# Output projection of a recurrent segment loop: its last blocks by column halves, and the segment's end spread over the next step

## The chip, the cores and the metric

The kernel runs on one core of a Trainium2 chip, whose engines are TensorE (matmuls and transposes, into PSUM), VectorE, ScalarE, GpSimd and SyncE, the last of which here only issues DMA transfers. Time is device time in microseconds (us) of one execution; the figure quoted for a kernel is the median of its runs.

## The reference, cut to what matters

Two independent parts are computed and set side by side in the output's columns. Part B is a long convolution (state space model); it comes first in the kernel and is not touched. Part A is an attention layer that runs over segments, and each segment needs the result of the one before:

```python
for s in range(n_seg):                                  # 64 segments of 32 rows
    h = jnp.concatenate([mem, x[:, 32*s:32*s+32]], axis=1)   # 8 memory rows + 32 rows, 1024 wide
    q, k, v = (einsum('btd,dhe->bhte', h, W) for W in (Wq, Wk, Wv))   # 32 heads of 128
    p = softmax(where(mask, einsum('bhqe,bhke->bhqk', q, k) * scale, -1e9))
    o = einsum('bhte,hed->btd', einsum('bhqk,bhke->bhqe', p, v), Wo)
    mem = o[:, :8]                                      # memory of the next segment
    outs.append(o[:, 8:])
```

All data are bf16, sums are kept in f32.

## The kernel before

**The recurrent rows.** Only 32 of a segment's 40 rows depend on the loop: the 8 memory rows and 24 of the 32 others are the columns of `hT` (1024 as 8 blocks of 128 partitions, 32 columns each; columns 24 to 31 hold the memory). The remaining 8 rows of each segment ("left") have their keys, queries and values made ahead of the loop and kept in DRAM (`PKd`, `VXd`); what the attention gives for them (the left products) is written to `OLd` in each step and projected after the loop, for all segments at once.

**One step.** `part_a` (L233) runs 64 steps. The order of all instructions on every engine is written out by hand in the source: each engine executes its instructions in that order, and waits where data is not there. A step projects K, Q of the first half of the heads (t = 0), K, Q of the second (t = 1), then V of both (`quads`, L358: eight blocks of weights each; four matmuls of 512 columns run side by side on four column groups of TensorE); ScalarE copies each result from PSUM to SBUF (`evac`, L369). Between them stand the transposes of K and Q (`tr`, L374), the scores (L387), the softmax (`below`, `powers`, `weigh`, `turn`, L404 to L425, VectorE and ScalarE), the spreading of the probabilities over block-diagonal tiles (L427 to L440, VectorE and GpSimd) and the product with V (`pv`, L442). `evac_o` (L458) copies that product to `o0` and `o1`, and `oproj` (L467) multiplies it with the sixteen blocks of Wo, blocks 0 to 7 from `o0`, 8 to 15 from `o1`. An even block reads the first half of `o0` or `o1` (two of its four heads), an odd block the second half. The sum stands in `pp[:, 1, :]`, as four row groups of 256 columns.

**The end of a step (L563 to L583).** ScalarE copies the sum to `ob` in two halves of 128 columns (L567), TensorE forms the left product of t = 1 (`pv_l`), then transposes both halves (L573), VectorE writes the memory columns of `hT` from them (L575), even 128-blocks of `hT` from the first half and odd ones from the second. The next step's first matmul (block 0 of K) needs `hT`. Then VectorE fetches the weight block `("k", 0, 7)`, and ScalarE copies the two left products (L578, L581), with the load of the next step's `PKd` rows (L327) between them, and issues two stores (L343, L347).

**Weights.** Most of the 64 blocks of 512 KB are resident in SBUF. Twelve are streamed from DRAM in every step by SyncE's queue through four slots (`stage`, L294): `STREAM` names nine, `STREAM_O` blocks 4, 8, 13 of Wo. A slot is reloaded as soon as TensorE has read it for the last time. Three blocks (`KEPT`: K 7, half of Q 7, half of Wo 15) live in PSUM as raw bits and are fetched by VectorE into SBUF in each step (`fetch`, L311; `words`, L291), in pieces of at most 512 columns.

**The arena.** Almost all of a step's small tiles share one SBUF area of 5984 bytes a partition. `AT` gives each tile's byte address; tiles whose lives do not overlap lie on each other, and a write into a place waits for the reads of what lay there.

Of the kernel before, what the change touches and what calls it, by code (L numbers as in the profile page):

```python
# [11 lines left out]
F32 = mybir.dt.float32  # L12
# [20 lines left out]
SLOTS = 4  # L33

ARENA = 5984
AT = {"K7a": 3072, "K7b": 1024, "K7c": 2048, "K7d": 4192, "ob": 4960, "pk": 0, "vx": 3392, "Q7a": 2048, "Q7b": 3072,
# [3 lines left out]


def weight_blocks(Wq, Wk, Wv, Wo):
# [190 lines left out]
def part_a(ctx, tc, x, src, WD, HE, seg_len, out_a, ahead, W_res, rest, places, first):  # L233
# [27 lines left out]
    def unit(key):  # L261
        if key in rest:

            rest.remove(key)
            load_resident(tc, wres, src, key, W_res, None, places.pop(0)() if places else None)
        if key in W_res:
            return W_res[key]
        if key in KEPT:
            return ahead_of.pop(key) + halves.get(key, [])
        between.pop(key, lambda: None)()  # L270
        if key in first:
            return first.pop(key)
        return stage(key, WD[key][:])
# [8 lines left out]
    def at(name, *dims):  # L282

        n = int(np.prod(dims))
        t_ = arena[:, AT[name] // 2:AT[name] // 2 + n]
        if len(dims) == 1:
            return t_
        names = "abc"[:len(dims)]
        return t_.rearrange("p (%s) -> p %s" % (" ".join(names), " ".join(names)), **dict(zip(names, dims)))

    def words(out, in_):  # L291
        nc.vector.tensor_scalar(out=out.bitcast(I32), in0=in_.bitcast(I32), scalar1=0, scalar2=None, op0=ALU.bitwise_or)  # L292
# [7 lines left out]
    def load_kept(key):  # L300
        t_ = first.pop(key) if key in first else stage(key, src(key))
        kept[key] = {}
        for n in (1,) if key in HALF else (0, 1):
            kept[key][n] = ps_k.tile([128, 512], F32, name="keep", tag="keep%d" % sum(len(b) for b in kept.values()))
            words(kept[key][n][:], t_[:, 1024 * n:1024 * n + 1024])
        if key in HALF:
            t_ = ahead.low["half"] if key[0] == "q" else wres.tile([128, 1024], BF16, name="Whalf")
            nc.sync.dma_start(out=t_[:], in_=src(key)[:, 0, :] if key[0] == "o" else src(key)[:, 0:1024])
            halves[key] = [(0, 1024, t_)]

    def fetch(key):  # L311

        ahead_of[key] = []
        for name, lo, n in KEPT[key]:
            t_ = at(name, n) if name else S_[:, 0:n]
            words(t_, kept[key][lo // 1024][:, lo % 1024 // 2:(lo % 1024 + n) // 2])
            ahead_of[key].append((lo, n, t_))

    def columns(w, lo, n):

        if not isinstance(w, list):
            return [(0, w[:, lo:lo + n])]
        return [(max(lo, l_) - lo, t_[:, max(lo, l_) - l_:min(lo + n, l_ + n_) - l_]) for l_, n_, t_ in w if l_ < lo + n and lo < l_ + n_]

    def load_pk(j):
        pk = at("pk", 512)
        nc.scalar.dma_start(out=pk, in_=PKd[j])  # L327
        return pk
# [23 lines left out]
    load_kept(("k", 0, 7))  # L352
    fetch(("k", 0, 7))
    pk = load_pk(0)
    between["q", 0, 2] = lambda: load_kept(("q", 0, 7))
    between["v", 0, 7] = lambda: load_kept(("o", 15))
    for s in range(NS):
        def quads(m, t, kcs, a=None):  # L358
            if a is None:
                a = ps.tile([128, 512], F32, name="acc", tag=BANK[m, t])  # L360
            for kc in kcs:
                w = unit((m, t, kc))
                for g in range(4):
                    for o_, rhs in columns(w, 512 * g, 512):
                        nc.tensor.matmul(a[32 * g:32 * g + 32, o_:o_ + rhs.shape[1]], lhsT=hT[:, kc, :], rhs=rhs,  # L365
                                         start=(kc == 0), stop=(kc == KC - 1), tile_position=(0, 32 * g), skip_group_check=True)
            return a
# [87 lines left out]
            pv(p[:], t, V, pb.rearrange("p a b c -> p a (b c)"), lbs)  # L455
            return p

        def evac_o(p, name):  # L458
            o = at(name, 4, 4, SL)
            nc.scalar.copy(out=o, in_=p[:].rearrange("p a (g q) -> p a g q", g=4))  # L460
            return o

        def pv_l(pl, t, V, L):

            pv(pl, t, V, L[:, 0].rearrange("p (a b) k -> p a (b k)", a=4), [L[:, 1].rearrange("p a k -> p (a k)")])

        def oproj(po, us, oT):  # L467
            for u in us:
                w = unit(("o", u))
                for hh in range(2):  # L470
                    h = 2 * u + hh
                    for qt in range(4):
                        for o_, rhs in columns(w, 1024 * hh + 256 * qt, 256):
                            nc.tensor.matmul(po[32 * qt:32 * qt + 32, o_:o_ + rhs.shape[1]], lhsT=oT[:, h % 4, (h % 16) // 4, :], rhs=rhs,  # L474
                                             start=False, stop=(h == 31), tile_position=(0, 32 * qt), skip_group_check=True)

        a = quads("k", 0, (0, 2, 4, 6, 1, 3, 5, 7))
        k0 = evac(a, "k0")
        a = quads("q", 0, range(0, 6))
        fetch(("q", 0, 7))  # L480
# [74 lines left out]
        powers(sc1, 1)  # L555
        oproj(pp[:, 1, :], range(0, 5), o0)
        pv1 = pv_x(1, V1, pb1, [lb1])
        o1 = evac_o(pv1, "o1")
        lt1 = turn(weigh(sc1, 1, "ln1"), "lt1")
        oproj(pp[:, 1, :], range(5, 8), o0)  # L560
        L1 = left_blocks(lt1[:, 0:4, :], lt1[:, 4, :], "L1")
        fetch(("o", 15))
        oproj(pp[:, 1, :], range(8, 16), o1)  # L563
        ob = at("ob", 2, 256)
        osb = ob[:, 0, :]
        for j in range(2):
            nc.scalar.copy(out=osb[:, 128 * j:128 * j + 128], in_=pp[:, 1, 128 * j:128 * j + 128])  # L567
        pl = ps.tile([128, 4, 32], F32, name="pl", tag="b2")
        pv_l(pl[:], 1, V1, L1)
        if s + 1 < NS:  # L570
            pt_o = [ps.tile([128, 4, SL], BF16, name="tro", tag=tag) for tag in ("b0", "b1")]
            for j in range(2):
                nc.tensor.transpose(out=pt_o[j][:].rearrange("p a b -> p (a b)"), in_=osb[:, 128 * j:128 * j + 128], identity=ident[:])  # L573
            for j in range(2):
                nc.vector.tensor_copy(out=hT[:, :, XM:SL].rearrange("p (q j) r -> p j q r", j=2)[:, j], in_=pt_o[j][:, :, XM:SL])  # L575
        if s + 1 < NS:
            fetch(("k", 0, 7))
        nc.scalar.copy(out=ob[:, 1, 0:128], in_=pp[:, 0, 0:128])  # L578
        if s + 1 < NS:
            pk = load_pk(s + 1)  # L580
        nc.scalar.copy(out=ob[:, 1, 128:256], in_=pl[:].rearrange("p a k -> p (a k)"))  # L581
        if s + 1 < NS:
            stores(s, ob)  # L583

    order = sorted(range(16), key=lambda u: ("o", u) not in W_res)
    wo = {}
# [933 lines left out]
```

## Time and profile before

| | |
|---|---|
| median of 3 runs | 2079.41 us (2068.97 to 2083.44) |
| the profiled execution's own time | 2084.53 us |
| its span, first to last instruction | 2082.8 us |
| mean granted TensorE clock | 0.978, 1.00 from 800 to 2000 us |
| DMA: moved in all | 590.77 MB, 284 GB/s on average |
| streamed loads of the loop (wst from WD) | 768 blocks of 512 KB |
| PKd and VXd loads, OLd and out stores in each step | 128, 112, 64 and 64 KB |

How to read the lines that follow. PE is TensorE, PEld its weight loads, DVE VectorE, ACT ScalarE, POOL GpSimd, SP SyncE; a "q" behind a name is the issue of a DMA on that engine. L12 is line 12 of the kernel. Groups of lines name output and input tiles, partitions x elements and type. A line of the timeline has its start in us, its length, engine, line, operation, tiles, count, and in brackets how long the engine had been idle before and which instruction ended that. The chain of work that ended last follows each instruction back to what released it. The busy time of stretches gives each engine's busy us in each stretch in the order PE, PEld, DVE, ACT, POOL, then granted clock, DMA share, GB/s. A line of the waits has the waiting engine and line, what ended the wait, us in total, times, the longest.

The loop fills the time from about 700 to 2020 us; what lies before is part B and the making of the left rows' keys and values, what lies after the projection of the left products.

### The profile page before, as it was taken

Reading aid. Unit: us, or ns where it says so; the run is one execution under the profiler, and the core shown is the slowest. Engines: PE = TensorE matmul, PEld = TensorE weight load, DVE = VectorE, ACT = ScalarE, POOL = GpSimd, SP = SyncE. Lnnn points to the kernel's source line nnn. Section 1 sums busy time; section 2 is a strip of 40 time slices with the busy share of each in tenths; the row PEclk is TensorE's granted clock in tenths of the full one; section 3 lists DMA queues with packets and bytes.
Section 4 is the critical chain, followed back from the end, with each engine's and each line's share of the span. In section 5 each row is a group of like instructions: output and inputs, shape, how many; then the busy total and the mean of one; then the engine's idle time right before and its main releaser. Section 6 shows DMA issues by size and latency. Waiting matters only on the chain.

```text
span 2082.8 us, 78569 instructions
## 1 busy us (share of the span) xinstructions
PE 1877.7 (90%) x33734; PEld 1188.9 (57%) x33734; DVE 1417.1 (68%) x3352; ACT 1047.5 (50%) x1917; POOL 402.5 (19%) x780
## 2 busy tenths in 40 slices
PE   2699999978999679999999999999999999999989
PEld 1365665756888435555555555555555555555554
DVE  8689999889899246665656656666566666666650
ACT  5899999951333234444444444444444444444430
POOL 2133443452010111111111111111111111111121
PEclk9999999989999779999999999999999999999999
DMA  7696985665635799999999999999999999999991
GB/s 192 179 255 205 266 234 167 167 207 185 217 131 179 288 339 341 343 339 336 336 328 325 334 327 344 337 335 340 331 342 343 336 340 345 334 341 345 332 334 49
DMA packets 344017, 590.77 MB, mean 284 GB/s; under 512 B 108536, under 2 KB 220184, under 8 KB 341620
## 3 DMA queue, kind: packets, MB, share of 16 engines
q1 hardware_dynamic: 297016, 528.00, 74.5%
q0 software_dynamic: 10544, 33.69, 4.8%
q10 hardware_dynamic: 36108, 24.07, 3.7%
q8 instruction: 264, 4.33, 0.8%
q14 instruction: 85, 0.70, 0.1%
HBM read 530.86 MB, written 65.26 MB: 286 GB/s over the span
## 4 chain that ended last, share of the span: by engine, by line
PE 34%; DMA 23%; DVE 4%; issue 2%; ACT 2%; POOL 0%; ACTq 0%; SPq 0%; POOLq 0%; DVEq 0%
PE acc L365 20%; PE pp L474 6%; DMA wst<-WD_o 6%; DMA wst<-WD_v 5%; DMA arena<-PKd 5%; DMA wst<-WD_q 3%; PE pe L610 3%; DMA wst<-WD_k 2%; PE tr L376 2%; PE sc L390 1%; DMA W_o<-in_A_Wo_dram 1%; DVE arena L432 1%; ACT arena L460 1%; DVE sc L407 1%; PE pv L444 0%
## 5 line engine op out<-in xcount | busy, mean ns | idle before, releaser
L365 PEld LDWEIGHTS <-a_hT 128*32 128x32 bf16 x12352 | 342.3, 96 | 302.4 <-issue 56.6
L371 ACT CAST arena<-acc 128x512 bf16<-128x512 f32 x384 | 225.1, 586 | 408.0 <-PE acc L365 348.8
L365 PE MATMUL acc<-W,a_hT 128*32 128x512 bf16 x4864 | 377.1, 383 | 0.3 <-issue 0.3
L474 PEld LDWEIGHTS <-arena 128*32 128x32 bf16 x8256 | 210.3, 97 | 107.7 <-ACT arena L460 52.1
L365 PE MATMUL acc<-wst,a_hT 128*32 128x512 bf16 x2304 | 232.7, 383 | 23.8 <-DMA wst<-WD_v 11.3
L292 DVE TENSOR_SCALAR arena<-keep 128x256 int32<-128x256 int32 (+1 forms) x512 | 176.3, 396 | 39.5 <-PE acc L365 36.8
L474 PE MATMUL pp<-W_o,arena 128*32 128x256 bf16 x4608 | 174.3, 275 | 6.5 <-DMA W_o<-in_A_Wo_dram 6.2
L365 PE MATMUL acc<-MF,a_hT 128*32 128x512 bf16 x2048 | 172.3, 383 | 0.0
L379 POOL COPY arena<-arena 128x128 bf16<-128x128 bf16 x128 | 37.6, 294 | 685.9 <-DMA arena<-PKd 309.9
L414 DVE TENSOR_REDUCE a_mx<-sc 128x4 f32<-128x160 f32 (+1 forms) x192 | 73.0, 380 | 82.2 <-ACT sc L410 82.2
L167 PE MATMUL pro<-xTl,wsl 128*128 128x512 bf16 x512 | 119.0, 383 | 9.5 <-ACT xTl L111 5.1
L406 DVE TENSOR_REDUCE a_mx<-sc 128x4 f32<-128x160 f32 (+1 forms) x192 | 71.9, 375 | 78.9 <-PE sc L394 77.6
L1059 PEld LDWEIGHTS <-MF 128*128 128x128 bf16 x1024 | 102.8, 101 | 30.1 <-issue 8.7
L410 ACT ACTIVATE sc<-sc 128x160 f32<-128x160 f32 (+1 forms) x192 | 63.9, 333 | 102.6 <-DVE sc L407 80.1
L437 POOL TENSOR_TENSOR arena<-arena,a_BD 128x128 bf16<-128x128 bf16 x128 | 69.2, 541 | 226.5 <-DVE arena L424 209.8
L489 DVE COPY arena<-tr 128x512 bf16<-128x512 bf16 x64 | 27.2, 425 | 126.0 <-PE tr L376 126.0
L1059 PE MATMUL hps<-KT,MF 128*128 128x256 bf16 x720 | 94.7, 284 | 14.2 <-DVE x L1228 11.2
L567 ACT CAST arena<-pp 128x128 bf16<-128x128 f32 x128 | 27.8, 269 | 154.9 <-PE pp L474 154.9
L1285 PE MATMUL yp<-Bt,MI 128*128 128x256 bf16 x680 | 104.5, 275 | 0.8 <-ACT yb L1301 0.8
L460 ACT CAST arena<-pv 128x512 bf16<-128x512 f32 x128 | 75.3, 588 | 56.7 <-PE pp L444 42.4
L1097 ACT ACTIVATE E<-pa 128x648 bf16<-128x648 f32 x128 | 91.4, 714 | 17.0 <-PE pa L1089 10.1
L474 PE MATMUL pp<-wst,arena 128*32 128x256 bf16 x1536 | 76.9, 277 | 19.6 <-DMA wst<-WD_o 11.8
(314 smaller groups left out, 3971.8 us busy)
## 6 DMA issues: line engine op xcount, KB each, us to landing
wst<-WD_v SPq DMA_DIRECT2D x256, 512.0 KB
wst<-WD_k SPq DMA_DIRECT2D x192, 512.0 KB
wst<-WD_o SPq DMA_DIRECT2D x192, 512.0 KB
wst<-WD_q SPq DMA_DIRECT2D x128, 512.0 KB
Ud<-ux POOLq DMA_DIRECT2D x16, 1024.0 KB, 5.4
uq<-Ud SPq DMA_DIRECT2D x32, 512.0 KB
wsl<-in_A_Wk_dram SPq DMA_DIRECT2D x16, 512.0 KB
wsl<-in_A_Wv_dram SPq DMA_DIRECT2D x16, 512.0 KB
```

The source lines that it names most:

```text
L167: nc.tensor.matmul(a[:], lhsT=w[:, kc, 128 * j:128 * j + 128], rhs=xTl[:, kc, :, :].rearrange("p s k -> p (s k)"), start=(kc == 0), stop=( ...
L292: nc.vector.tensor_scalar(out=out.bitcast(I32), in0=in_.bitcast(I32), scalar1=0, scalar2=None, op0=ALU.bitwise_or)
L365: nc.tensor.matmul(a[32 * g:32 * g + 32, o_:o_ + rhs.shape[1]], lhsT=hT[:, kc, :], rhs=rhs, start=(kc == 0), stop=(kc == KC - 1), tile_pos ...
L371: nc.scalar.copy(out=q, in_=a[:])
L406: nc.vector.tensor_reduce(out=m_, in_=x, axis=AX.X, op=ALU.max)
L414: nc.vector.tensor_reduce(out=m_, in_=x, axis=AX.X, op=ALU.add)
L437: nc.gpsimd.tensor_tensor(out=L[:, 0].rearrange("p (a b) k -> p a b k", a=4), in0=bc(lt[:, :, 0:XL].unsqueeze(2), [128, 4, 4, XL]), in1=bc ...
L460: nc.scalar.copy(out=o, in_=p[:].rearrange("p a (g q) -> p a g q", g=4))
L474: nc.tensor.matmul(po[32 * qt:32 * qt + 32, o_:o_ + rhs.shape[1]], lhsT=oT[:, h % 4, (h % 16) // 4, :], rhs=rhs, start=False, stop=(h == 3 ...
L1059: pe.matmul(s_[r][half][:, cs, :], lhsT=MF[:, kc, 4 * rr + mc, cs, :], rhs=rhs, start=(i == 0 and mc == 0), stop=(i == 1 and mc == 3), ski ...
L1097: sc.activation(out=T["E", r, e // 4][:, lo:lo + 8 * NE].rearrange("p (i c) -> p i c", i=2), in_=T.pop(("p", r, e))[:, :, 0:4 * NE], func= ...
L1285: pe.matmul(yp[:, b, :], lhsT=m_[:, b, cs, kc, :], rhs=Bt[:, kc, j, half, c_, :], start=(kc == 0 and cs == 0 and half == 0), stop=(kc == 3 ...
```

## The change

The last three blocks of Wo (now 11, 13, 15) are multiplied by column halves. Columns 0 to 127 go to `pp` as before; columns 128 to 255 go to a tile of their own in another PSUM bank (`rest_o`), and what the earlier blocks had summed there is copied to SBUF (`base`, f32) and added by VectorE. Blocks of the second half of the heads run in the order 8, 10, 12, 14, 9, then 11, 13, 15, and `o1` is copied in two halves. The first half of the result is transposed at the end of the step; the second (`memory(1)`) in the next step, behind the first block of K, in a tile shared with the left product of t = 1 (`last`). The left products are copied, and the two stores issued, in the next step too. The block `("k", 0, 7)` is fetched by ScalarE in its last three pieces, and by VectorE in the first two, one ahead of and one behind `memory(1)`; the load of `PKd` stands behind ScalarE's pieces. All arena tiles have new places.

```diff
-AT = {"K7a": 3072, "K7b": 1024, "K7c": 2048, "K7d": 4192, "ob": 4960, "pk": 0, "vx": 3392, "Q7a": 2048, "Q7b": 3072,
-      "k0": 1024, "q0": 3328, "KT0": 2048, "QT0": 1024, "k1": 1024, "q1": 4288, "pn0": 5312, "pt0": 2304, "KT1": 1024,
-      "QT1": 4288, "pb0": 4448, "V0": 1024, "L0": 5472, "o0": 2048, "V1": 1024, "pn1": 3072, "pt1": 4288, "pb1": 0,
-      "lb1": 4960, "ln1": 0, "lt1": 704, "L1": 2048, "o1": 3936, "Oa": 4960, "Ob": 2560}
+AT = {"K7a": 3072, "K7b": 0, "K7c": 4864, "K7d": 4096, "ob": 2048, "pk": 1024, "vx": 4352, "Q7a": 3072, "Q7b": 4960,
+      "k0": 0, "q0": 4352, "KT0": 3072, "QT0": 0, "k1": 3072, "q1": 0, "pn0": 2048, "pt0": 5344, "KT1": 3072, "QT1": 0,
+      "pb0": 3072, "V0": 2048, "L0": 0, "o0": 3072, "V1": 0, "pn1": 5248, "pt1": 5664, "pb1": 1024, "lb1": 2048,
+      "ln1": 2048, "lt1": 2368, "L1": 3072, "o1": 4960, "Oa": 1024, "Ob": 3584}
...
+    def fetch_bits(eng, key, pieces):
+        for name, lo, n in pieces:
+            t_ = at(name, n) if name else S_[:, 0:n]
+            bits = kept[key][lo // 1024][:, lo % 1024 // 2:(lo % 1024 + n) // 2]
+            if eng is nc.vector:
+                words(t_, bits)
+            else:
+                eng.copy(out=t_, in_=bits.bitcast(BF16))
+            ahead_of[key].append((lo, n, t_))
...
+    def memory(j):
+        nc.tensor.transpose(out=tr_o[j].rearrange("p a b -> p (a b)"), in_=osb[:, 128 * j:128 * j + 128], identity=ident[:])
+        nc.vector.tensor_copy(out=hT[:, :, XM:SL].rearrange("p (q j) r -> p j q r", j=2)[:, j], in_=tr_o[j][:, :, XM:SL])
+
+    def left_out():
+        nc.scalar.copy(out=ob[:, 1, 128:256], in_=last[:, 0:128])
+        nc.scalar.copy(out=ob[:, 1, 0:128], in_=pp[:, 0, 0:128])
...
-        def evac_o(p, name):
-            o = at(name, 4, 4, SL)
-            nc.scalar.copy(out=o, in_=p[:].rearrange("p a (g q) -> p a g q", g=4))
+        def evac_o(p, name, parts=1):
+            o, n = at(name, 4, 4, SL), 4 // parts
+            for i in range(0, 4, n):
+                nc.scalar.copy(out=o[:, i:i + n], in_=p[:, i:i + n, :].rearrange("p a (g q) -> p a g q", g=4))
             return o
...
+        def oblock(po, u, w, oT, lo, n, start=False):
+            for hh in range(2):
+                h = 2 * u + hh
+                for qt in range(4):
+                    for o_, rhs in columns(w, 1024 * hh + 256 * qt + lo, n):
+                        nc.tensor.matmul(po[32 * qt:32 * qt + 32, o_:o_ + rhs.shape[1]], lhsT=oT[:, h % 4, (h % 16) // 4, :], rhs=rhs,
+                                         start=start and hh == 0, stop=(h == 31), tile_position=(0, 32 * qt), skip_group_check=True)
...
-        a = quads("k", 0, (0, 2, 4, 6, 1, 3, 5, 7))
+        a = quads("k", 0, (0,))
+        if s:
+            fetch_bits(nc.vector, ("k", 0, 7), KEPT["k", 0, 7][0:1])
+            memory(1)
+            fetch_bits(nc.vector, ("k", 0, 7), KEPT["k", 0, 7][1:2])
+            left_out()
+            stores(s - 1, ob)
+        quads("k", 0, (2, 4, 6, 1, 3, 5, 7), a)
...
-        o1 = evac_o(pv1, "o1")
+        o1 = evac_o(pv1, "o1", 2)
...
         fetch(("o", 15))
-        oproj(pp[:, 1, :], range(8, 16), o1)
+        oproj(pp[:, 1, :], (8, 10, 12, 14, 9), o1)
         ob = at("ob", 2, 256)
-        osb = ob[:, 0, :]
-        for j in range(2):
-            nc.scalar.copy(out=osb[:, 128 * j:128 * j + 128], in_=pp[:, 1, 128 * j:128 * j + 128])
-        pl = ps.tile([128, 4, 32], F32, name="pl", tag="b2")
-        pv_l(pl[:], 1, V1, L1)
+        osb, base = ob[:, 0, :], ob[:, 1, :].bitcast(F32)
+        ends = [(u, unit(("o", u))) for u in (11, 13, 15)]
+        for u, w in ends:
+            oblock(pp[:, 1, 0:128], u, w, o1, 0, 128)
+        nc.scalar.copy(out=osb[:, 0:128], in_=pp[:, 1, 0:128])
+        nc.scalar.copy(out=base, in_=pp[:, 1, 128:256])
+        rest_o = ps.tile([128, 128], F32, name="po", tag="b2")
+        for u, w in ends:
+            oblock(rest_o[:], u, w, o1, 128, 128, u == 11)
+        last = ps.tile([128, 512], F32, name="pl", tag="b1")
         if s + 1 < NS:
-            pt_o = [ps.tile([128, 4, SL], BF16, name="tro", tag=tag) for tag in ("b0", "b1")]
-            for j in range(2):
-                nc.tensor.transpose(out=pt_o[j][:].rearrange("p a b -> p (a b)"), in_=osb[:, 128 * j:128 * j + 128], identity=ident[:])
-            for j in range(2):
-                nc.vector.tensor_copy(out=hT[:, :, XM:SL].rearrange("p (q j) r -> p j q r", j=2)[:, j], in_=pt_o[j][:, :, XM:SL])
+            tr_o = [ps.tile([128, 4, SL], BF16, name="tro", tag="b0")[:], last[:, 256:320].bitcast(BF16).rearrange("p (a b) -> p a b", a=4)]
+            memory(0)
+        pv_l(last[:, 0:128].rearrange("p (a k) -> p a k", a=4), 1, V1, L1)
+        nc.vector.tensor_tensor(out=osb[:, 128:256], in0=rest_o[:], in1=base, op=ALU.add)
         if s + 1 < NS:
-            fetch(("k", 0, 7))
-        nc.scalar.copy(out=ob[:, 1, 0:128], in_=pp[:, 0, 0:128])
-        if s + 1 < NS:
+            ahead_of["k", 0, 7] = []
+            fetch_bits(nc.scalar, ("k", 0, 7), KEPT["k", 0, 7][2:])
             pk = load_pk(s + 1)
-        nc.scalar.copy(out=ob[:, 1, 128:256], in_=pl[:].rearrange("p a k -> p (a k)"))
-        if s + 1 < NS:
-            stores(s, ob)
+        if s + 1 == NS:
+            left_out()
```

More of the change, by code (lines that the diff above doesn't have):

```diff
@@ L465, in pv_l @@
             pv(pl, t, V, L[:, 0].rearrange("p (a b) k -> p a (b k)", a=4), [L[:, 1].rearrange("p a k -> p (a k)")])
+        def oblock(po, u, w, oT, lo, n, start=False):
[5 more added lines that the diff above has]
+                                         start=start and hh == 0, stop=(h == 31), tile_position=(0, 32 * qt), skip_group_check=True)
         def oproj(po, us, oT):
             for u in us:
[L469 to L475, printed above, removed]
-        a = quads("k", 0, (0, 2, 4, 6, 1, 3, 5, 7))
+                oblock(po, u, unit(("o", u)), oT, 0, 256)
+        a = quads("k", 0, (0,))
[6 more added lines that the diff above has]
+        quads("k", 0, (2, 4, 6, 1, 3, 5, 7), a)
         k0 = evac(a, "k0")
```

## The prediction

> **What bounds the kernel now.** First the page: busy shares, slices, the chain that ended last.
>
> ```profile
> PE 1877.7 (90%) x33734; PEld 1188.9 (57%) x33734; DVE 1417.1 (68%) x3352; ACT 1047.5 (50%) x1917; POOL 402.5 (19%) x780
> DMA  7696985665635799999999999999999999999991
> PE 34%; DMA 23%; DVE 4%; issue 2%; ACT 2%; POOL 0%; ACTq 0%; SPq 0%; POOLq 0%; DVEq 0%
> PE acc L365 20%; PE pp L474 6%; DMA wst<-WD_o 6%; DMA wst<-WD_v 5%; DMA arena<-PKd 5%; DMA wst<-WD_q 3%; PE pe L610 3%; DMA wst<-WD_k 2%; PE tr L376 2%; PE sc L390 1%; DMA W_o<-in_A_Wo_dram 1%; DVE arena L432 1%; ACT arena L460 1%; DVE sc L407 1%; PE pv L444 0%
> ```
>
> From slice 15 on (the loop of 64 segments, 62 full steps of 20.02 us on average by the starts in the trace) the DMA row stands at 9, and the chain alternates between matmuls (L365, L474) and loads: streamed weights, and the small PKd load. Three stretches of the loop, each engine's busy time, then clock, DMA share and rate:
>
> ```profile
> 800.00:1200.00 400.00, 376.92 (x8442) 220.40 (x8445) 248.84 (x775) 177.89 (x398) 57.58 (x138) 1.00 0.95 334
> 1200.00:1600.00 400.00, 379.64 (x8536) 223.57 (x8532) 250.98 (x784) 178.52 (x400) 57.61 (x141) 1.00 0.95 337
> 1600.00:2000.00 400.00, 380.34 (x8539) 223.28 (x8531) 250.14 (x783) 178.75 (x403) 59.23 (x142) 1.00 0.95 338
> ```
>
> TensorE and the DMA engines are both at 95%: a step moves 6.73 MB, which at a share of 1.00 would take 0.947 x 20.02 = 18.96 us. So neither alone sets the step. By phase of the step the DMA share is 0.97 to 1.02 in the third to the twelfth twentieth and 0.87 to 0.94 in the last seven: up to the scores of t=1 the loads are late, after them a chain of engines sets the pace. The end of one step shows that chain (start, us, engine, line, idle before):
>
> ```profile
> 1219.33 0.31 DVE L406 TENSOR_REDUCE a_mx<-sc 128x4 f32<-128x160 f32 x1
> 1220.04 0.29 ACT L410 ACTIVATE sc<-sc 128x160 f32<-128x160 f32 x1 [1.14 <-DVE sc L407]
> 1220.43 0.59 ACT L460 CAST arena<-pv 128x512 bf16<-128x512 f32 x1
> 1221.07 0.40 PE L474 MATMUL pp<-wst,arena 128*32 128x256 bf16 x8 [0.24 <-ACT arena L460]
> 1221.76 0.65 DVE L292 TENSOR_SCALAR arena<-keep 128x256 int32<-128x256 int32 x2
> 1222.33 0.21 DVE L292 TENSOR_SCALAR a_S<-keep 128x64 int32<-128x64 int32 x1
> 1222.78 0.22 PE L474 MATMUL pp<-a_S,arena 128*32 128x128 bf16 x1
> 1223.09 0.27 ACT L567 CAST arena<-pp 128x128 bf16<-128x128 f32 x1 [2.07 <-PE pp L474]
> 1223.15 0.32 ACTq L327 DMA_DIRECT2D arena<-PKd  x1
> 1223.41 0.40 PE L573 MATMUL tro<-a_ident,arena 128*128 128x128 bf16 x2
> 1223.68 0.34 DVE L575 COPY a_hT<-tro 128x32 bf16<-128x32 bf16 x2 [1.14 <-PE tro L573]
> 1223.90 0.40 PE L365 MATMUL acc<-Wlow,a_hT 128*32 128x512 bf16 x4
> ```
>
> VectorE's maxima (L406) release the exponential, ScalarE then copies o1 in one piece (L460), and TensorE takes up the output blocks 0.64 us after that copy begins. VectorE meanwhile fetches block 15 from PSUM (L292). After the last output matmul (1222.78) TensorE does little for 1.12 us: copy at +0.30, transposes at +0.62, hT copy at +0.89, next step's first matmul at +1.12. One more wait matters:
>
> ```profile
> POOL arena L379 <- DMA arena<-PKd: 303.6, 46, 7.7
> ACT arena L567 <- PE pp L474: 136.5, 60, 3.8
> ```
>
> In 46 of 60 steps the packed K/Q rows (PKd) land last of all that GpSimd's put_kl (L379) waits for. Issued 0.75 us ahead of the step's first matmul, they land 5.04 us behind it on average, and the scores (L390) can start 0.49 us later; that cost TensorE 0.11 us a step.
>
> [...] both L573 stand between L448 and L365, each in order. [...] PKd lands 0.17 us after the streamed block k1:5 that was issued 0.54 us before it, and over 55 steps the two landings correlate at 0.93. [...] L437 takes 0.40 us alone and 0.77 beside VectorE's L432/L429; L429 then 0.55 instead of 0.42.
>
> **The change part by part**, per step. E is the last output matmul of before; times in ScalarE's and VectorE's order are counted from the last matmul of the left half (in before, from E). I take the spacings of before's instructions, over all steps of the trace.
>
> *o1 by halves.* ScalarE copies 512 columns in 0.59 us, 128 in 0.27; by the line between them 256 take 0.38. The four even units need only the first half, so TensorE resumes 0.21 us earlier; the second half ends at 0.75, long before the unit that needs it (four units of 0.218 us later). **-0.21**.
>
> *Column halves.* A group of four 256-column matmuls starts every 109 ns, one of 128 columns every 56 ns (the last two L474 of the step), so splitting adds 3 ns to six groups, **+0.02**. The six groups of the right half (0.34 us) now run behind the left half's copy (0.62 us from its last matmul to the transposition): **-0.34** at best. pv_l, 0.23 us, stays under cover of the hT copy.
>
> *What holds these two back.* Already the left half of unit 15 needs VectorE's second piece (Ob). It ends at E-0.25 in the median step, never later than E-0.18, while TensorE would come to it at E-0.60. Taking for each step the later of E-0.59 and the end of Ob plus 0.07, the left half's last matmul comes 0.31 us before E on average: 0.12 in the 29 of 63 steps where VectorE sets it, up to 0.59 in those delayed by loads. Then L0: its new place lies on QT1, so GpSimd starts it after the scores, beside VectorE's L429; by the contended row that delays VectorE by 0.12 us, in half the steps, 0.06 on average. Gain of the end: 0.31 - 0.06 = **-0.25**.
>
> *The right half's transposition in the next step.* The median gap into a group of transposes is 0.312 us where 0.213 is the stream before it, and out of it 0.149: 0.25 us of TensorE for one. **+0.25**. Its operand (the addition: after the hT copy at +0.89, spacing 0.17, and 0.33 as L417, the nearest row) is there at about +1.40 of the left half's end; TensorE asks at 1.12 + 0.31 = 1.43. Odd blocks are read three units later (0.64 us), VectorE's K7a piece (0.38) and the hT copy fit in. Cover gone, each 0.1 us late is 0.1 us of step.
>
> *K7's last three pieces on ScalarE, left_out and stores in the next step.* ScalarE: copies at 0.30 and 0.46, K7c from 0.70 to 1.19, K7d to 1.57, the last to 1.84, the two left products to about 2.4, two store issues (0.33 and 0.57) to about 3.4; k0's copy is due at 3.45. It is hidden by k0's own eight units; if not, the tr(k0) that waits for it comes some 2 us later. The base copy takes the place of the second half's copy. VectorE is spared 0.95 us where it wasn't late: 0. The stores leave ob 1.15 us later, which pn0 now overwrites at +9.0 of the step; at 6 to 7 us of flight some four steps in 60 wait, as three did for q1's copy: 0, at worst +0.05.
>
> *PKd's load* is moved behind K7d's copy. K7d lies on vl, so it waits for pv_l's last matmul: by 0.30 us from matmul to ScalarE and 0.06 to the issue, PKd leaves 0.07 us **after** the step's first matmul instead of 0.75 before, 0.82 us later. Queued behind that wait are the left products and the stores; put_kl, then the scores, wait for the landing. Two bounds. If the flight of 5.8 us follows the issue, scores wait 0.50 us a step instead of 0.11 (each step's landing shifted by 0.82, TensorE's arrival by 0.25): +0.39. If landing goes by the queue of streamed loads, as the 0.93 says (with the time between the two issues the flight correlates at 0.05), it comes after k1:5 as now: 0, or -0.05, since TensorE comes later. First packets follow an issue by 2.77 us, so they'd be in the engines at +2.84, and k1:1 before k1:5 lands at +2.95: I take the second and **+0.05**. Unit 13's slot is freed some 0.5 us later, its load k1:5 issued as much later; that load too then waits its turn behind k1:1, so 0, and up to +0.1.
>
> **Sum.** -0.25 + 0.02 + 0.25 + 0.05 = +0.07 us a step; by 63 steps +4 us. The profiled execution took 2084.5 us (span 2082.8), so 2089; the runs' median, 2079.4, stands 5 below it: **2083**.
>
> **Rivals.** *PKd becomes the bound* (slower). Its landing follows its issue; decisive once it lands later than 5.4 us into the step. +0.39 in place of +0.05: +0.41 a step, +26 us, 2105; with the late k1:5 on top 2111. For it: 46 of 60 waits at put_kl already end with PKd. Against: the correlation. *The end's gain stays whole* (faster): the loads that delay TensorE are earlier requested, VectorE's chain isn't what holds the left half. -0.55 + 0.27 - 0.11 (the PKd wait gone, as TensorE comes later) = -0.39, -25 us, 2055. For it: half the steps end long after Ob. Against: in these the loads are late, and they stay 95% busy. *Nothing moves*, since the loads set the step: 18.96 us are needed in any case, TensorE's gain becomes waits for wst: 2079, inside the forecast.
>
> **How the numbers follow.** Forecast, the last rival included, 0.57, with its own range 2066 to 2098 (a quarter of a microsecond a step either way); PKd 0.25; gain whole 0.18. One per cent, 20.8 us, is about what a measurement of this kernel can tell from no change. Faster by over 1% is the third case, slower the second. The range leaves a tenth on each side: 2055 to 2110.
>
> **What would show it.** Right: the next step's first matmul about 0.87 us after the left half's end plus the right half, VectorE's Ob directly ahead of unit 15; PKd's landing still near 5.1 us. Wrong: idle TensorE before L390 growing by a third of a microsecond (PKd), the transposition of the right half waiting for the addition, ScalarE late with k0, or a DMA share of 0.97 and more at a shorter step.

## The result, and the profile after

| | before | after |
|---|---|---|
| median | 2076.85 us (4 runs, one more than above; 2068.97 to 2083.44) | 2108.38 us (4 runs, 2102.69 to 2112.18) |
| profiled execution, its span | 2084.53, 2082.8 us | 2109.67, 2108.0 us |
| clock from 800 to 2000 us | 1.00 | 0.99 to 1.00 |

The ratio is 1.0145, with a 95% interval of 1.012 to 1.0171: slower by 1.45%, where no change was forecast. The time lies inside the range, near its upper end, but for a reason that the prediction does not contain: that it lies inside is luck.

First the page of after: busy shares, DMA by slices, the queue that carries instructions.

```profile
PE 1898.7 (90%) x35206; PEld 1197.6 (57%) x35206; DVE 1367.3 (65%) x3227; ACT 1123.6 (53%) x2170; POOL 388.4 (18%) x780
DMA  7696985756645899999999999999999999999991
q8 instruction: 276, 4.52, 0.9%
```

TensorE executes 1472 matmuls more (35206 against 33734), 23 in each of 64 steps, and as many weight loads; VectorE has less to do and ScalarE more, as the change says. Queue q8, which the profile lists as "instruction" and the prediction does not mention, has 276 packets of 16 KB: one for each 255.1 of the 70412 matmuls and weight loads. In before, with 67468 of them (255.6 a packet), it had

```profile
q8 instruction: 264, 4.33, 0.8%
```

The same three stretches of the loop as in before (busy us of PE, PEld, DVE, ACT, POOL, then clock, DMA share, GB/s):

```profile
800.00:1200.00 400.00, 377.45 (x8691) 220.24 (x8684) 225.73 (x713) 196.81 (x465) 51.67 (x134) 0.99 0.93 326
1200.00:1600.00 400.00, 381.39 (x8912) 221.72 (x8914) 231.55 (x736) 200.69 (x477) 53.12 (x140) 1.00 0.94 334
1600.00:2000.00 400.00, 375.42 (x8732) 219.36 (x8723) 229.83 (x724) 197.38 (x466) 52.19 (x137) 1.00 0.94 328
```

The DMA engines are a little less busy and move less per second than before (0.95, 334 to 338), so transfers did not become the bound. The time of a step, from the starts of instructions in the two traces (mean of 55 steps, us):

| from ... to ... | before | after | change |
|---|---|---|---|
| first matmul of the step, scores of t = 0 | 5.78 | 6.28 | +0.50 |
| scores of t = 0, scores of t = 1 | 5.11 | 5.10 | -0.01 |
| scores of t = 1, first matmul of the next step | 9.13 | 8.97 | -0.16 |
| sum | 20.02 | 20.35 | +0.33 |

+0.33 us in 63 steps is 21 us of the 25 by which the spans differ; the first steps, left out here, differ by more (over 61 steps, all but the first two and the last, the step is 0.45 us longer). The end of a step in after, from the copy of o1 on (start, us, engine, line, idle before):

```profile
1207.26 0.65 ACT L481 CAST arena<-pv 128x256 bf16<-128x256 f32 x2
1208.61 0.65 DVE L292 TENSOR_SCALAR arena<-keep 128x256 int32<-128x256 int32 x2
1209.09 0.23 PE L493 MATMUL pp<-Whalf,arena 128*32 128x128 bf16 x4
1209.18 0.21 DVE L292 TENSOR_SCALAR a_S<-keep 128x64 int32<-128x64 int32 x1
1210.14 0.40 PEld L493 LDWEIGHTS <-arena 128*32 128x32 bf16 x28 [1.00 <-issue]
1210.14 0.24 PE L493 MATMUL pp<-arena 128*32 128x128 bf16 x4 [0.82 <-DVE a_S L292]
1210.21 0.28 PE L493 MATMUL po<-W_o,arena 128*32 128x128 bf16 x8
1210.80 0.23 PE L368 MATMUL tro<-a_ident,arena 128*128 128x128 bf16 x1
1211.23 0.33 ACTq L338 DMA_DIRECT2D arena<-PKd  x1
1211.29 0.40 PE L385 MATMUL acc<-Wlow,a_hT 128*32 128x512 bf16 x4
1211.62 0.23 PE L368 MATMUL pl<-a_ident,arena 128*128 128x128 bf16 x1
```

From the right half's last matmul to the next step's first take 0.8 us (about 0.87 was named), and the right half's transposition follows the first block. But in the middle of block 15 TensorE stands still for a microsecond. The line names VectorE's fetch; yet VectorE ended at 1209.39, 0.75 us before TensorE went on. The weight load, which waits for nothing of block 15, says "issue": it waited for nothing that the profile shows. Those waits of weight loads in before, from 860 to 2020 us (engine, line, us in total, times, longest):

```profile
PEld L365 <- issue: 38.0, 71, 3.2
PEld L474 <- issue: 31.8, 93, 1.8
```

and in after:

```profile
PEld L385 <- issue: 49.2, 90, 1.7
PEld L493 <- issue: 45.4, 125, 2.5
```

They sum short ordinary gaps and these long ones. The long ones have a place. Counted in instructions of TensorE, those of after stand 256 apart (128 matmuls with their weight loads), and drift by 2 from step to step. A step has 896 matmuls and weight loads in the trace, and 3.5 x 256 is 896 too; the drift comes of two semaphore instructions of TensorE, which the trace has at L410 and L464 in each step (114 from 860 to 2020 us). Counted with them, a step has 898 instructions, and the long waits keep one place in each 256 through the loop. In the trace, exactly one 16 KB packet of q8 arrives between two such places (198 packets in 198 intervals from 860 to 2020 us, 189 in 189 in before), and no such place is passed less than 1.2 us after its packet has arrived. The 36 places of after at which more than 0.3 us were lost were all passed 1.2 to 1.6 us after it, the others 2.3 us after it in the median. No view shows what a packet holds. The reading that these counts and times give, used from here on, is that q8 brings TensorE's instructions in pieces of 256, one ahead, and that TensorE stands still where a piece has come late. Before the stop above, a packet landed at 1208.67, 1.47 us ahead of the first matmul behind it. The piece arrives this long after the place before it was passed (median, and the 90th percentile): 3.5 and 4.5 us in before, 3.5 and 4.6 in after. The intervals themselves are 6.0 and 5.8 us in the median; their shortest tenth is below 5.2 in before, below 5.0 in after.

The time lost at these places in those 61 steps, as excess over the median of the same instruction in other steps, us a step (such a sum is uncertain by some 0.04, by how near to a place an excess is counted):

| | before | after | change |
|---|---|---|---|
| first matmul to scores of t = 0 | 0.03 | 0.21 | +0.18 |
| scores of t = 0 to t = 1 | 0.03 | 0.07 | +0.04 |
| scores of t = 1 to the next step | 0.17 | 0.35 | +0.18 |
| sum (places with over 0.1 us) | 0.24 (33 of 202) | 0.63 (58 of 214) | +0.39 |

Over the same 61 steps the step is 0.45 us longer, so 0.39 is most of it; over the 55 steps of the table before, the stalls rise by about 0.33 us of +0.33. The same sum taken at places shifted along the stream of instructions gives about 0.03 us, so it is these places that count.

### The profile page after: what moved, and what is told of

It is laid out like the page before. It is cut to its first block, busy times and chain, and to the rows that moved or that the text cites. A ratio compares the mean times of both kernels' runs of the same rounds, so it can differ in the third digit from the quotient of the medians.

```text
span 2108.0 us, 82150 instructions
## 1 busy us (share of the span) xinstructions
PE 1898.7 (90%) x35206; PEld 1197.6 (57%) x35206; DVE 1367.3 (65%) x3227; ACT 1123.6 (53%) x2170; POOL 388.4 (18%) x780
## 5 line engine op out<-in xcount | busy, mean ns | idle before, releaser
L385 PE MATMUL acc<-W,a_hT 128*32 128x512 bf16 x4864 | 382.1, 383 | 1.5 <-issue 1.1
L493 PEld LDWEIGHTS <-arena 128*32 128x32 bf16 x9728 | 219.8, 97 | 120.7 <-issue 69.2
L385 PE MATMUL acc<-wst,a_hT 128*32 128x512 bf16 x2304 | 239.5, 385 | 22.9 <-DMA wst<-WD_v 12.7
L292 DVE TENSOR_SCALAR arena<-keep 128x256 int32<-128x256 int32 (+1 forms) x386 | 143.2, 398 | 85.5 <-PE acc L385 82.0
L493 PE MATMUL pp<-W_o,arena 128*32 128x256 bf16 x4608 | 156.4, 269 | 5.9 <-DMA W_o<-in_A_Wo_dram 5.9
L457 POOL TENSOR_TENSOR arena<-arena,a_BD 128x128 bf16<-128x128 bf16 x128 | 51.5, 403 | 310.7 <-DVE arena L444 214.3
L481 ACT CAST arena<-pv 128x256 bf16<-128x256 f32 (+1 forms) x192 | 79.1, 449 | 36.7 <-PE pp L464 26.9
L167 PEld LDWEIGHTS <-wsl 128*128 128x128 bf16 x512 | 50.4, 98 | 73.0 <-issue 19.5
L452 DVE TENSOR_TENSOR arena<-arena,a_BDL 128x384 bf16<-128x384 bf16 (+1 forms) x128 | 80.9, 632 | 14.1 <-POOL arena L399 9.7
```

What stands on the lines that cost most here:

```text
L167: nc.tensor.matmul(a[:], lhsT=w[:, kc, 128 * j:128 * j + 128], rhs=xTl[:, kc, :, :].rearrange("p s k -> p (s k)"), start=(kc == 0), stop=( ...
L452: eng.tensor_tensor(out=out, in0=bc(pl.unsqueeze(1), [128, m, n]), in1=bc(BDL[:].rearrange("p a b -> p (a b)")[:, j:j + m].unsqueeze(2), [ ...
L481: nc.scalar.copy(out=o[:, i:i + n], in_=p[:, i:i + n, :].rearrange("p a (g q) -> p a g q", g=4))
```

## The experiments

Four theories are weighed. **F**: the change is slow because TensorE's instructions come late; it has 46 more a step, in the densest stretch. **S**: the rebuilt end itself is longer. **K**: the later PKd load is at fault. **V**, formed on the way: VectorE's chain up to its fetch of block 15 holds the last block. "Stalls" below are the sum at the places described.

**The column halves alone, in the kernel before.**

```diff
...
-        oproj(pp[:, 1, :], range(8, 16), o1)
+        oproj(pp[:, 1, :], range(8, 13), o1)
+        ends = [(u, unit(("o", u))) for u in (13, 14, 15)]
+        for lo in (0, 128):
+            for u, w in ends:
+                oblock(pp[:, 1, lo:lo + 128], u, w, o1, lo, 128)
```

> The kernel before, with one edit: its last three blocks (13, 14, 15) are multiplied by column halves into the same bank, 23 matmuls and their 23 weight loads more in a step, everything else as it was. Theory F (TensorE waits for its own instructions, which come in pieces of 256 by DMA; the trace of after has 0.63 us of such stalls a step, that of before 0.24): 25 us slower than before, between 15 and 30, and stalls of about 0.6 us a step. Theory S (what costs is the rebuilt end itself: the right half's transposition, VectorE's fetch of block 15): 1 us slower (0.02 us a step). Theory K (the later PKd load): no change.

Measured: 2108.01 us, ratio 1.0132 (1.0104 to 1.0161); stalls 0.52 us a step. This part of the change (here with blocks 13, 14 and 15, both halves in one bank) adds 23 matmuls and their weight loads and nothing else, and costs as much as all of it. It also makes TensorE ask earlier for block 15's pieces; what that costs is measured further below.

**The change without the column halves** (blocks 11, 13, 15 whole, the second half copied as before).

```diff
-            oblock(pp[:, 1, 0:128], u, w, o1, 0, 128)
+            oblock(pp[:, 1, :], u, w, o1, 0, 256)
...
-        nc.scalar.copy(out=base, in_=pp[:, 1, 128:256])
-        rest_o = ps.tile([128, 128], F32, name="po", tag="b2")
-        for u, w in ends:
-            oblock(rest_o[:], u, w, o1, 128, 128, u == 11)
+        nc.scalar.copy(out=osb[:, 128:256], in_=pp[:, 1, 128:256])
...
-        nc.vector.tensor_tensor(out=osb[:, 128:256], in0=rest_o[:], in1=base, op=ALU.add)
```

> The kernel after, with blocks 11, 13 and 15 whole again (one sum in one bank, both halves copied by ScalarE, no addition); all the rest as in after: o1 by halves, the right half's transposition in the next step, left products and stores there, PKd's load behind ScalarE's pieces, the new places. Theory F: stalls as before; the transposition's 0.25 us less 0.1 for o1 remain, 9 us slower than before, about 2086. Theory S: the cover that the split gave is lost too, 0.3 us a step, about 2125. Theory K: as after, 2108.

Measured: 2087.66 us, ratio 1.0038 (1.0021 to 1.0055); stalls 0.16. This is F's forecast; S and K missed. So 21 of the 29 us (against a kernel before of 2079.09 in this comparison) go with the column halves.

**PKd's load ahead of ScalarE's pieces of K 7, in after.**

```diff
-            fetch_bits(nc.scalar, ("k", 0, 7), KEPT["k", 0, 7][2:])
             pk = load_pk(s + 1)
+            fetch_bits(nc.scalar, ("k", 0, 7), KEPT["k", 0, 7][2:])
```

> The kernel after, with PKd's load issued ahead of ScalarE's three K7 pieces, so about 0.4 us earlier in the step. Theory F, and landing by the queue of streamed loads: no change from after, 2108 within 5. Theory K: scores start up to 0.3 us earlier in each step, 15 to 20 us faster than after.

Measured: 2122.18 us, ratio 1.0198 (1.0161 to 1.0235), no faster at all: K falls. The load, issued 0.5 us earlier than in after, landed no earlier. F, which allowed 5 us either way, missed too: that the kernel is 14 us slower than after isn't explained. Its profiled execution was its shortest, 2109.02 us, and looks like after's (stalls 0.52).

**Fewer TensorE instructions in after.**

```diff
-            for hl in range(4):
+            for hl in range(1):
                 for g in range(4):
```

> The kernel after, with 24 of the 32 small matmuls for the left rows' scores left out in each step (three of four heads a group: the left rows' attention of those heads is not computed), so that TensorE has as many instructions a step as before (850 against 852). They take some 5.6 ns each, 0.13 us a step, 8 us in all. Theory F: the stalls go back to 0.25 us a step, so 33 us faster than after, about 2075. Theories S and K: 8 us faster than after, about 2100.

Measured: 2096.81 us, ratio 1.0095 (1.0058 to 1.0132), stalls 0.34 to 0.38: between the theories, nearer to S and K. The count alone does not rule. By position in the step, the stalls near the scores, where the matmuls were taken out, have gone (in before they averaged 0.55 us a place in one stretch of 16 matmuls there), while those of the last 60 matmuls are at 0.18 us a step, after's being 0.24 and before's 0.04. F has to be put as a matter of pace: a stretch stalls that uses up a piece faster than the next one comes (in after 3.5 us after the place before, in the median). This kernel's profiled execution (2107.27 us) was the longest of its four, and the rest of its step was some 0.2 us above after's; why stays open.

**As many instructions more, elsewhere** (six q blocks of t = 0 by column halves, in before).

```diff
-                for g in range(4):
-                    for o_, rhs in columns(w, 512 * g, 512):
+                n = 256 if (m, t) == ("q", 0) and 1 <= kc <= 6 else 512
+                for lo, g in [(lo, g) for lo in range(0, 512, n) for g in range(4)]:
+                    for o_, rhs in columns(w, 512 * g + lo, n):
```

> The kernel before with six q blocks of t = 0 (kc 1 to 6) taken by column halves, 24 matmuls and 24 weight loads more a step, as many as the change adds, but in blocks of 512 columns, where TensorE's instructions are only half as dense in time as in the output blocks. Theory F by count (each further instruction costs its share of fetching, wherever it stands): 2098 to 2108 us, stalls 0.45 us a step or more. Theory F by density (only a stretch that uses up 256 instructions faster than the next 256 come stalls): 2076 to 2088 us, stalls 0.2 to 0.35 us a step.

Measured: 2088.7 us, ratio 1.0043 (1.003 to 1.0057), stalls 0.44. Halves of 512 columns are only as dense as whole output blocks (by before and after, a group of four starts every 109 ns with 256 columns, every 216 with 512), and the stalls moved with them: of the 0.44, 0.23 lie between the two scores, right behind the split blocks, and 0.03 in the last 60 matmuls. But only some 8 us come of it. The step without its stalls took 19.6 us where before's took 19.8, in a profiled execution that was this kernel's shortest (2082.77 us). In this stretch the streamed loads are late (a DMA share of 0.97 to 1.02 there in before), so a stall there can take the place of a wait that would follow; that is argued from the sums, not shown by itself. So neither count nor density alone gives the price: where the stall falls matters too.

**Half of each streamed load, in before and in after.**

```diff
-        return stage(key, WD[key][:])
+        t_ = wst.tile([128, 2048], BF16, name="wst", tag="w%d" % (loads[0] % SLOTS))
+        loads[0] += 1
+        nc.sync.dma_start(out=t_[:, 0:1024], in_=WD[key][:, 0:1024])
+        return [(1024 * i, 1024, t_[:, 0:1024]) for i in range(2)]
```

> The kernel before, but every streamed weight block is loaded only by its first half (256 KB instead of 512 KB) and the matmuls of the second half read the first half again, so the arithmetic of those blocks is left out in part while TensorE executes as many instructions of the same shapes. What it takes away is load on the DMA engines. Theory F (TensorE's instructions come in pieces of 256 over DMA engines that the weights keep busy, and a piece that is asked for in a dense stretch comes late): the stalls at the piece boundaries fall from 0.24 us to below 0.1 us a step, and with the waits for streamed blocks gone the kernel takes 2040 to 2065 us. Theory S (the end of the step itself sets the difference): any time, but the same difference to its twin with the change as between after and before.

> The same halving of the streamed loads, in the kernel after. Theory F: the stalls at the piece boundaries fall from 0.63 us to below 0.15 us a step, and the kernel is no more than 8 us slower than the halved kernel before, or up to 10 us faster, where after stands 29 us above before. Theory S: it is 20 us or more slower than the halved kernel before, as the code of the end of the step is the same and no load is late in either.

Measured: 2025.49 us (2023.03 to 2029.44) for the halved before, 2039.97 (2037.9 to 2042.86) for the halved after. The stalls fall to 0.01 us a step in both, with pieces arriving 1.8 and 2.0 us after the place before (median) and a DMA share of 0.61 and 0.62 from 860 to 2020 us, where before and after have 0.95 and 0.94: the late pieces went with busy DMA engines, as F says. The halved before is faster than the 2040 to 2065 us that F gave it. But the halved after is still 14.5 us slower, which F did not allow and S put at 20 or more. Both miss. With nothing late the path itself is longer. The three parts of the step tell where (us, mean):

| | first matmul to scores 0 | to scores 1 | to the next step | sum |
|---|---|---|---|---|
| halved before | 5.51 | 5.00 | 8.66 | 19.17 |
| halved after | 5.79 | 4.94 | 8.66 | 19.39 |

The transposition moved to the next step costs its 0.28 us, and the end that should pay for it gains nothing. The halved before, from the scores of t = 1:

```profile
1206.41 0.28 PE L393 MATMUL sc<-arena 128*32 128x40 bf16 x16
1206.84 0.42 DVE L432 TENSOR_TENSOR arena<-arena,a_BDx 128x512 bf16<-128x512 bf16 x1 [0.36 <-PE sc L397]
...
1213.65 0.21 DVE L295 TENSOR_SCALAR a_S<-keep 128x64 int32<-128x64 int32 x1
...
1213.85 0.28 PE L477 MATMUL pp<-arena 128*32 128x256 bf16 x4
```

and the halved after:

```profile
1211.83 0.28 PE L413 MATMUL sc<-arena 128*32 128x40 bf16 x16
...
1212.41 0.45 DVE L452 TENSOR_TENSOR arena<-arena,a_BDx 128x512 bf16<-128x512 bf16 x1 [0.68 <-PE sc L417]
...
1218.64 0.65 DVE L295 TENSOR_SCALAR arena<-keep 128x256 int32<-128x256 int32 x2
...
1219.07 0.50 PE L496 MATMUL pp<-arena 128*32 128x128 bf16 x4
...
1219.21 0.21 DVE L295 TENSOR_SCALAR a_S<-keep 128x64 int32<-128x64 int32 x1
1219.35 0.34 PE L496 MATMUL po<-W_o,arena 128*32 128x128 bf16 x8
```

VectorE's work between scores and block 15 is the same chain, but it begins 0.58 us after the scores instead of 0.43 (0.16 later in the median step), and its last piece starts 7.38 instead of 7.24 us after them. In the halved after, the four matmuls of block 15's last part take 0.50 us from first to last, where they take 0.23 when the piece Ob is there (the end listed below): they wait for Ob, which VectorE's second copy (L295) has ready at 1219.29. By the addresses, pb0 (the tile that L432 and L452 write) lay on QT1 and now lies on KT1, which the left scores (L397, L417) read last; that this is what delays it was not tried alone, and the profile names the left scores as the end of the wait in both.

**The column halves alone, with halved loads; and block 15's pieces on ScalarE, in the halved after.** The first is the first experiment's edit with the one above. The second:

```diff
-        fetch(("o", 15))
+        ahead_of["o", 15] = []
+        fetch_bits(nc.scalar, ("o", 15), KEPT["o", 15])
```

> The kernel before with blocks 13, 14 and 15 by column halves, its streamed blocks loaded by their first half only (their second half is read from the first again, so those products are not the reference's). With the loads halved no stall at a piece boundary is left, so only the path of the split itself shows. Theory F alone (the split costs nothing but fetching): 2023 to 2029 us, as the halved kernel before. Theory V (the left half of block 15 asks 0.3 us earlier for the piece Ob that VectorE fetches, waits for it, and the right half then runs behind that wait): the last output matmul comes 0.2 us later, 2034 to 2040 us.

> The kernel after with halved streamed loads, as above, and with block 15's three pieces (Oa, Ob and the short one) copied from PSUM by ScalarE, behind its copy of o1's second half, instead of by VectorE. Theory V (VectorE's chain from the scores of t = 1 to Ob sets the end of the step in the kernel after): the left half no longer waits, 0.25 to 0.33 us less a step, 2019 to 2025 us. Theory S (what the end does after the left half sets it: copy, transposition, copy): 2036 to 2042 us as without it.

Measured: 2038.4 us (2037.15 to 2045.93) and 2019.87 us (2014.67 to 2020.64). V holds in both: the split alone lengthens the path by 13 us, its last output matmul coming 0.21 us later after the scores; and with the pieces on ScalarE the path is 20 us shorter, 5.6 us below the halved before. The end of that kernel:

```profile
1205.22 1.00 ACT L330 COPY arena<-keep 128x512 bf16<-128x512 bf16 x2
1206.07 0.32 ACT L330 COPY a_S<-keep 128x128 bf16<-128x128 bf16 x1
...
1206.51 0.23 PE L496 MATMUL pp<-arena 128*32 128x128 bf16 x4
1206.56 0.28 PE L496 MATMUL po<-W_o,arena 128*32 128x128 bf16 x8
```

ScalarE has the pieces ready at 1206.39, before TensorE asks, and the right half follows at once.

**The same edit in the complete kernel after.**

> The kernel after, complete, with block 15's three pieces copied by ScalarE instead of VectorE. With halved loads this took 20 us off. The two causes add up (path and late instructions, half each): 2108 less 20 is 2088, that is 5.6 us below the kernel before by the path and 14 us above it by the stalls, 2081 to 2092 us, with stalls at the piece boundaries still 0.5 to 0.75 us a step. If late instructions alone made the kernel after slow: 2100 to 2110 us. If the path alone did: 2068 to 2078 us.

Measured: 2102.46 us (6 runs, 2097.96 to 2108.87), ratio 1.0105 (1.0074 to 1.0137). Only 6 of the 20 us show: the time lies where late instructions alone put it, and not where the sum of both causes does. This is the run that weighs them. Its path is shorter than that of the kernel before, by the halved kernels; with the full loads it is 22 us slower than before. TensorE's waits for late instructions have grown to 0.78 us a step, 0.54 above before, while its waits for streamed blocks have not grown: in the waits from 860 to 2020 us, with the columns as above,

```profile
PE acc L385 <- DMA wst<-WD_v: 6.6, 13, 1.0
PE pp L493 <- DMA wst<-WD_o: 6.3, 10, 1.1
PE acc L385 <- DMA wst<-WD_k: 2.5, 4, 1.0
```

where before had

```profile
PE acc L365 <- DMA wst<-WD_v: 10.9, 15, 2.9
PE pp L474 <- DMA wst<-WD_o: 9.9, 12, 1.6
...
PE acc L365 <- DMA wst<-WD_k: 4.2, 6, 1.0
```

The two causes do not add. The likely reason is that the wait for Ob and a late piece of instructions fall in the same stretch, and that the shorter path uses up its pieces faster; this was not tried by itself.

**A version without added instructions.** The kernel before with `o1` in two halves and the blocks in the order 8, 10, 12, 14, 9, 11, 13, 15; then the same with block 15's pieces on ScalarE.

```diff
-        o1 = evac_o(pv1, "o1")
+        o1 = evac_o(pv1, "o1", 2)
...
-        oproj(pp[:, 1, :], range(8, 16), o1)
+        oproj(pp[:, 1, :], (8, 10, 12, 14, 9, 11, 13, 15), o1)
```

> The kernel before with one part of the change alone: o1 copied in two halves, and the output blocks of t = 1 taken in the order 8, 10, 12, 14, 9, 11, 13, 15. No TensorE instruction is added. Theory F: 0.10 us less a step between o0's and o1's blocks and no more stalls, 6 us less in all: 2070 to 2078 us against a kernel before of 2078. Theory S (the new order of the blocks or the second copy costs something at the end): 2085 us or more.

> The kernel before with o1 copied in halves, its blocks in the order 8, 10, 12, 14, 9, 11, 13, 15, and block 15's three pieces copied by ScalarE instead of VectorE; no TensorE instruction added. Theory V: in undisturbed steps the last output matmul comes 0.15 us sooner (7.35 us after the scores of t = 1, where it is 7.50 with VectorE's Ob), some 6 us less than with o1's halves alone: 2066 to 2072 us. Theory F (a denser end runs into late instructions and gives it back): 2073 to 2080 us with stalls above 0.40 us a step.

Measured: 2075.97 us (22 runs), ratio 0.9983 (0.9965 to 1.0), and 2076.99 us (22 runs), ratio 1.0008 (0.9993 to 1.0022). At best 0.2% is gained. The stretch from the scores of t = 1 to the next step does become shorter, 8.86 and 8.77 us where before has 9.13, but the next step reaches its scores later, after 6.06 and 6.09 us instead of 5.78. In the first, whose profiled execution was the longest of its 22, some 0.1 us of that are stalls (0.3 to 0.4 us in the whole step). An earlier start also meets loads that are no earlier: where before waited 4.2 us for K's streamed blocks, these two wait

```profile
PE acc L365 <- DMA wst<-WD_k: 10.1, 16, 1.3
PE acc L365 <- DMA wst<-WD_k: 10.7, 19, 1.3
```

which is about 0.1 us a step; what makes up the rest stays open. The second, in which VectorE's chain no longer holds block 15, gains nothing on the first, though its stalls (0.20) are no higher than before's: V's price does not show in the complete kernel, and F's reason for that, more stalls, isn't seen in this one either.

## Why the prediction was wrong, point by point

- **Column halves, "+0.02"**: the step that failed. The spacing it used was right (109 and 56 ns a group, in after and in the halved kernels), but it priced 23 matmuls and 23 weight loads by their streaming only, as if instructions were always there. They use up TensorE's instruction pieces faster in the densest stretch of the step, while the DMA engines are 94% busy (from 860 to 2020 us). The missing term is +0.39 us a step, by 63 steps 25 us, and 2083 and 25 is 2108. That it comes out so exactly is luck, as the waits don't simply add: with halved loads, where no piece is late, the whole change still costs 14.5 us and the halves alone 13, by the wait for Ob.
- **Gain of the end, -0.25**: -0.16 measured in 55 steps, with about +0.08 us of stalls in the same steps, so about -0.24 without them, close to the forecast. But with halved loads, in undisturbed steps, it is zero, because the chain of VectorE that was named as the brake starts 0.16 us later than before; the prediction had 0.06 on average, from another cause (L0). The prediction gave the steps that VectorE sets 0.12 us and those delayed by loads up to 0.59; that the delayed steps make up the -0.24 would fit, but was not separated. The part named "-0.34 at best" is there as such: from the last output matmul to the next step 0.78 instead of 1.12 us in the halved kernels.
- **o1 by halves, -0.21**: the gap ahead of o1's blocks fell from 0.50 to 0.34 us in the halved kernels, -0.16; but counted from the scores, o1's first block starts at 5.79 us in both. VectorE's delay had taken it away ahead of it.
- **The right half's transposition, +0.25**: 0.28, both in the complete kernels' shortest steps (5.51 and 5.79 us to the scores) and in the halved ones. Right.
- **K 7's pieces, left products and stores on ScalarE, 0**: right; in undisturbed steps the time to the scores grows by the transposition and no more.
- **PKd, +0.05**: right. Issued 0.06 us ahead of the step's first matmul instead of 0.75, it lands at 5.32 us instead of 5.04, again with a correlation of 0.93 to k1:5, and the scores wait 0.05 us more a step. The rival that put the loss here named about the right time (2105) for a wrong reason, and moving the load forward didn't help.
- **The rival that the loads set the step** was nearer the truth for one half: an earlier end is given back in the first stage (the kernels without added instructions show part of it). The waits put down to "issue" and q8 stood in the profile of before, with 0.24 us a step already lost; they were not priced.

## What to carry to other kernels

Count what a rearrangement adds in instructions, not only in columns. Where the DMA engines are nearly full, look for the queue of instructions and for waits that the profile puts down to "issue", find their spacing in instructions, and compare the time that the densest 256 instructions take with the time that the next piece needs to come (in after 3.5 us in the median, 4.6 at the 90th percentile, and at least 1.2 more until TensorE passed into it). By an estimate from the 109 ns of a group of four, 256 instructions of whole output blocks take 3.5 us, and by half blocks, at 56 ns, 1.8. Halving the loads is a cheap way to see a path without this (0.01 us a step was left here), but what a path then gains need not show under full load (of 20 us here, 6 showed).

## What the runs showed of the hardware

- Queue q8 had 276 packets of 16 KB in after and 264 in before, one for each 256 instructions of TensorE, the semaphore instructions counted. From 860 to 2020 us exactly one landed between each two successive places 256 instructions apart: 3.5 us (median) after the first of the two was passed in before, with the DMA engines at 95%, 1.8 us in the halved before, with them at 61%. In before and in after TensorE passed no such place sooner than 1.2 us after its packet had come.
- Loss at these places was 0.01 us a step in before and after with halved loads, 0.24 in before, 0.63 in after, 0.78 in after with the shortest path (block 15's pieces on ScalarE).
- In after, four matmuls of 128 columns start every 56 ns, four of 256 every 109 ns. By these, blocks of 128 columns cost next to nothing in TensorE's own time, an estimate: twelve groups of four, 0.67 us, replace six, 0.65 us.
